# First token chunk multiplied among the last queries, token operands in two buffers of their own

## The chip, the cores and the metric

One core of one Trainium2 chip runs the whole program. The metric is the device time of one execution in microseconds; of several runs the median is given. A profiled execution of the same program supplies the trace.

## The reference, cut to what matters

Attention with random features, then a dense mixture of experts on its output. All matrices are float32.

```python
# q, k, v: (4, 8, 576, 64); omega: (128, 64); x: (2304, 512); w_gate: (512, 8)
# w1: (8, 512, 1024); w2: (8, 1024, 512)
h = einsum('bhsd,md->bhsm', x, omega) - sum(x*x)/2;  phi = exp(h - max(h)) / sqrt(m)
kv = einsum('bhsm,bhsd->bhmd', phi(k), v);  z = sum_s phi(k)
attn = einsum('bhsm,bhmd->bhsd', phi(q), kv) / (phi(q) . z + 1e-6)
x = attn reshaped to tokens x 512
P = exp(x @ w_gate - max);  8 times: P /= P.sum(1); P /= P.sum(0); P *= N / E
out = sum over e of P[:, e] * (relu(x @ w1[e]) @ w2[e])
```

## The kernel before, in words

**Attention.** A list of 36 jobs (lines 695 to 699) goes through keys, then keys mixed with queries, then the last queries. Each job is a generator; after each job is put in, `tick()` (L722) advances every open job by one stage. A stage is some 128-column transposes, matmuls of 65 to 256 columns, one or two PSUM evacuations on ScalarE (ACT) and some VectorE (DVE) work. The raw inputs lie in the pool `rw`, with three buffers each for `q`, `k` and `v` (L286). When the jobs are all in, `while active: tick()` (L750) lets the last queries run out.

**Token operands.** There are 18 tiles of 128 tokens in three chunks of six. When a chunk's six tiles stand in `xf`, `token_operands` (L98) makes seven operands for a seven-product (Strassen-like) 2x2 scheme, in the order 1, 5, 6, 3, 7, 2, 4 (`ORDER`). For each it forms a difference in place where one is needed (L107, on GpSimd (POOL) for chunks 0 and 1, on DVE for chunk 2), casts the high part on ACT (L122), takes the low part on DVE (L123), stores the pair to DRAM (L125, 768 KB), multiplies four of the seven by the gate weights `wgs` (`logits`, L147) and yields. The tile it writes is one of the four `xs` buffers (`token_tile`, L95). For chunk 2, whose tokens come last, the same tile is at once multiplied by the first expert's weights.

**Experts.** Sixteen units, each half an expert's hidden width. `first(u, c, i, g)` (L528) is a piece of the first product: six matmuls of 384 columns (L555) for one operand and one half of the weights, evacuated for each pair of pieces (L569 to L574). `second(s, i)` (L631) is six matmuls of 256 columns (L641) and one evacuation. A step `s` handles two token tiles: seven `second` calls, with pieces of later chunks taken from the list `todo` between them, five, five and four in three successive steps (L783). Left operands of a step come from `left_operands_a` and `left_operands_b` (L594, L610), on ACT and DVE. `split(u, w, i)` (L188) makes the high and low parts of a weight quarter: a difference on POOL (L194), a cast on ACT (L224), the low part on DVE or POOL (L225).

**The order of chunks.** The first unit takes chunk 2 first, from the buffers, then 0 and 1 (`order`, L506). Every later chunk's operands are read back from DRAM into `xs` by `load_next` (L514, L525), one for each pair of pieces done, four ahead.

**Between the two.** After the attention, left operands of step 0 are made, the query pool `sc` is closed, its memory goes to the pool `op_` (weight parts of the second product and the output tiles), four loads are issued (L759) and seven `split(0, 2, i)` follow (L761). `sc` lies on the side of memory that `op_` takes over, and `wgs` lies in `sc`. The pool `rw` gives its memory to `hp` (left operands and hidden tiles), the two PSUM banks of the key sums go to `px` (accumulators of `first`).

**What sets the order.** Line 825 builds the program with `schedule_with_timeline_sim=True`: a planner orders each engine's instructions by the order in the source and by when it thinks that each is ready. On the chip every engine, and the SP queue that issues the transfers, then works through its own list in order. Semaphores hold an instruction back until its inputs and its buffer are there.

Of the kernel before, what the change touches and what calls it, by code (L numbers as in the profile page):

```python
# [9 lines left out]
F32 = mybir.dt.float32  # L10
# [12 lines left out]
def moe_attention_kernel(  # L23
# [29 lines left out]
    P = 128  # L53
# [3 lines left out]
    SM = JM * P  # L57
    SR = S - SM
    XSB = 4
    RES = ()  # L60
    FB = 4
    NFB = FF // P // FB
# [35 lines left out]
    def token_operands(c, x):  # L98

        def q(r, h):  # L100
            h = 1 - h
            return x[:, 2 * r : 2 * r + 2, h * HL : (h + 1) * HL]

        last = c == NCH - 1

        def sub(o, a, b):
            (nc.vector if last else nc.gpsimd).tensor_tensor(o, a, b, op=ALU.subtract)  # L107

        for i in ORDER:
            if i == 5:
                sub(q(0, 0), q(0, 1), q(0, 0))
            elif i == 6:
                sub(q(0, 0), q(1, 1), q(0, 0))
            elif i == 7:
                sub(q(0, 1), q(1, 1), q(0, 1))
            elif i == 4:
                sub(q(0, 0), q(1, 0), q(0, 0))
            o = {3: q(1, 1), 7: q(0, 1), 2: q(1, 0)}.get(i, q(0, 0))  # L120
            t = token_tile()
            nc.scalar.copy(t[:, 0], o)  # L122
            nc.vector.tensor_tensor(t[:, 1], o, raw(t[:, 0]), op=ALU.subtract)  # L123
            xdram[c, i] = xd.tile([P, 2, 2, HL], F32, name=f"xd{c}_{i}")
            nc.sync.dma_start(out=xdram[c, i], in_=raw(t))  # L125
            logits(c, i, t)
            if last:
                xop[0, c, i] = t
                first(0, c, i, 0)
                first(0, c, i, 1)  # L130
            yield


    lpb = {}
# [127 lines left out]
    def load(which, key):  # L262

        src = {"q": q, "k": k, "v": v}[which]
        is_v = which == "v"
        if key[0] == "r":
            pr = key[1]
            rows = [(slice(i * SR, (i + 1) * SR), 2 * pr + i) for i in range(2)]
            if is_v:
                ts = []  # L270
                for i, (r, b) in enumerate(rows):
                    t = rw.tile([P, H + 1, D], F32, tag=f"vr{i}", bufs=1, name=f"vr{i}")
                    nc.gpsimd.memset(t, 0.0)
                    nc.gpsimd.memset(t[r, H, :], 1.0)
                    nc.sync.dma_start(out=t[r, :H, :], in_=src[b, :, SM:S, :].rearrange("h p d -> p h d"))
                    ts.append(t)
                rawt[which, key] = ts
            else:
                t = rw.tile([P, H, 1, D], F32, tag=f"{which}r", bufs=1, name=f"{which}r")
                for r, b in rows:  # L280
                    nc.sync.dma_start(out=t[r, :, 0, :], in_=src[b, :, SM:S, :].rearrange("h p d -> p h d"))
                rawt[which, key] = t
            return
        b, half = key
        view = src[b, :, :SM, :].rearrange("h (p j) d -> p h j d", j=JM)[:, :, 2 * half : 2 * half + 2, :]
        t = rw.tile([P, H + is_v, 2, D], F32, tag=which, bufs=3, name=which)  # L286
        if is_v:
            nc.gpsimd.memset(t[:, H], 1.0)
        nc.sync.dma_start(out=t[:, :H], in_=view)
        rawt[which, key] = t  # L290
# [214 lines left out]
    steps = [(u, n) for u in range(len(units)) for n in range(NP)]  # L505
    def order(u):  # L506

        return [NCH - 1] + list(range(NCH - 1)) if u == 0 else list(range(NCH))

    chunks = [(u, c) for u in range(len(units)) for c in order(u)]  # L510
    hraw, hneg, ops, xop, xres, hacc = {}, {}, {}, {}, {}, {}
    loads = [(u, c, i) for u, c in chunks[1:] for i in ORDER]

    def load_next():  # L514

# [12 lines left out]
    def first(u, c, i, g):  # L528
# [38 lines left out]
        if g == 1 or both is None:  # L567
# [4 lines left out]
                nc.vector.tensor_tensor(o, src, o, op=ALU.add)  # L572
            else:
                nc.scalar.copy(o, src)  # L574
        if g == 1 and (u, c) != chunks[0] and i not in RES:
            load_next()

    def tiles_of(u, n):
# [168 lines left out]
    hp_.append(ctx.enter_context(tc.tile_pool(name="hp", bufs=1, side="right", reuse_waits="tile")))  # L747
    kv_cm.__exit__(None, None, None)
    px.append(ctx.enter_context(tc.tile_pool(name="px", bufs=1, space=bass.MemoryType.PSUM, side="right")))
    while active:  # L750
        tick()
    left_operands_a(0)
    left_operands_b(0)
    sc_cm.__exit__(None, None, None)
# [1 line left out]
    ps[0] = ctx.enter_context(tc.tile_pool(name="ps4", bufs=4, space=bass.MemoryType.PSUM))  # L756
    pz.append(ctx.enter_context(tc.tile_pool(name="pz", bufs=1, space=bass.MemoryType.PSUM)))
    op_ = ctx.enter_context(tc.tile_pool(name="op", bufs=1, reuse_waits="tile"))
    for _ in range(XSB):  # L759
        load_next()  # L760
    for i in ORDER:  # L761
        split(0, 2, i)

    gate = sinkhorn()
    todo = pieces[14:]
    for s, (u, n) in enumerate(steps):
        c = n // (CT // 2)
        more = u + 1 < len(units)
# [10 lines left out]
        for k, i in enumerate(ORDER):  # L779
            second(s, i)  # L780
            if more and (n, k) in W2AT:
                split(u + 1, 2, ORDER[W2AT.index((n, k))])
            if k < (5, 5, 4)[n % 3] and todo:  # L783
                pc = todo.pop(0)
                first(*pc)
                j = ORDER.index(pc[2])
                if pc[1] == order(pc[0])[-1] and pc[3] == 1 and pc[0] + 1 < len(units) and j + 1 < len(ORDER):
                    split(pc[0] + 1, 1, ORDER[j + 1])
            if i == 7 and s + 1 < len(steps):
                left_operands_a(s + 1)  # L790
            if k in (1, 4):
                next(gate, None)
# [37 lines left out]
```

## Time and profile before

| what | value |
|---|---|
| median of 3 runs (lowest to highest) | 1658.14 us (1658.12 to 1659.32) |
| the profiled execution's own time | 1652.41 us |
| its span, first to last instruction | 1650.6 us |
| mean granted TensorE clock | 0.997 |

PE is TensorE's matmuls, PEld its weight loads. The page's first part gives busy time by engine; the span in 40 slices shows that only the first slice lies visibly below the others for PE. For this change the stretch from 110 us to 262 us matters: the three bursts of token operands and the change from attention to experts. The views used are busy time by stretch, waits, the timeline of one engine, groups of instructions and transfers.

### The profile page before, as it was taken

The numbers are of one execution on the slowest core, as the hardware profiler recorded it, in microseconds if no ns is written. First come the engines' busy times: TensorE is split into PE (matmuls) and PEld (weight loads), VectorE is DVE, ScalarE is ACT, GpSimd is POOL, SyncE is SP. The second block draws the span as 40 slices with busy tenths as digits, with TensorE's granted clock in tenths as the row PEclk, the third lists the DMA queues.
The fourth block names the chain that finished last, engine by engine and source line by source line (L and its number), as shares of the span: only waits on it lengthen the run. The fifth ranks groups of instructions, "written<-read, shape, count | busy, mean of one in ns | idle before, by whom it ended". The sixth has DMA issues, their size and how long they took to land.

```text
span 1650.6 us, 30079 instructions
## 1 busy us (share of the span) xinstructions
PE 1617.2 (98%) x11610; PEld 1598.3 (97%) x11610; DVE 1430.6 (87%) x2903; ACT 785.4 (48%) x1408; POOL 276.4 (17%) x232
## 2 busy tenths in 40 slices
PE   7999999999999999999999999999999999999998
PEld 7899889999999999999999999999999999999998
DVE  7999779898879898889888898989898888889878
ACT  6877646444334344443444443434444444444332
POOL 7631131111102011111111120102111111101000
PEclk9999999999999999999999999999999999999999
DMA  9422577564666565666647565665666565655462
GB/s 251 128 78 103 211 274 242 196 225 170 235 208 202 207 212 199 217 216 210 223 166 260 167 226 194 220 209 211 203 219 213 208 227 184 215 189 192 173 227 80
DMA packets 102686, 329.72 MB, mean 200 GB/s; under 512 B 14480, under 2 KB 39056, under 8 KB 102544
## 3 DMA queue, kind: packets, MB, share of 16 engines
q1 hardware_dynamic: 102544, 327.79, 58.1%
q8 instruction: 93, 1.52, 0.4%
q14 instruction: 49, 0.40, 0.1%
HBM read 306.53 MB, written 21.23 MB: 199 GB/s over the span
## 4 chain that ended last, share of the span: by engine, by line
PE 87%; DVE 11%; ACT 1%; issue 1%; SPq 0%; DMA 0%; POOL 0%; ACTq 0%; DVEq 0%
PE hx L555 24%; PE x L641 22%; PE hz L555 18%; PE z L641 11%; PE w L641 6%; DVE out L661 2%; DVE sm L592 1%; PE np L434 1%; DVE bl L592 1%; DVE mx L348 1%; PE kv L364 1%; PE qp L411 1%; DVE sl L620 1%; DVE cn L351 1%; PE pp L342 1%; DVE wl L225 1%
## 5 line engine op out<-in xcount | busy, mean ns | idle before, releaser
L555 PE MATMUL hx<-xs,wh 128*128 128x384 f32 x1536 | 371.9, 336 | 0.4 <-DVE prob L162 0.3
L661 DVE SCALAR_TENSOR_TENSOR out<-x,prob,out 128x256 f32<-128x256 f32 x504 | 237.0, 477 | 65.2 <-PE x L641 63.7
L555 PE MATMUL hz<-xs,wh 128*128 128x384 f32 x1152 | 282.0, 337 | 0.0
L555 PEld LDWEIGHTS hx<-xs,wh 128*128 128x128 f32 x1536 | 269.1, 188 | 0.8 <-issue 0.5
L194 POOL TENSOR_TENSOR st<-st 128x512 f32<-128x512 f32 x80 | 132.1, 1652 | 710.5 <-DVE wl L225 705.8
L555 PEld LDWEIGHTS hz<-xs,wh 128*128 128x128 f32 x1152 | 203.3, 189 | 0.2
L555 PE MATMUL hx<-xs,wl 128*128 128x384 f32 x768 | 199.6, 336 | 0.0
L623 ACT ACTIVATE bh<-hr 128x512 fp32r<-128x512 f32 x144 | 91.2, 633 | 223.5 <-PE x L641 218.4
L661 DVE SCALAR_TENSOR_TENSOR out<-z,prob,out 128x256 f32<-128x256 f32 x252 | 120.3, 477 | 56.8 <-PE z L641 56.2
L619 ACT CAST sh<-sm 128x512 fp32r<-128x512 f32 x144 | 89.6, 622 | 142.3 <-PE z L641 101.4
L224 ACT CAST wh<-st 128x512 fp32r<-128x512 f32 x176 | 104.8, 621 | 103.0 <-PE hx L555 43.1
L555 PE MATMUL hz<-xs,wl 128*128 128x384 f32 x576 | 151.2, 336 | 0.0
L592 DVE SCALAR_TENSOR_TENSOR sm<-hr,sm 128x256 f32<-128x256 f32 x288 | 137.4, 477 | 2.6
L555 PEld LDWEIGHTS hx<-xs,wl 128*128 128x128 f32 x768 | 138.7, 188 | 0.0
L225 DVE TENSOR_TENSOR wl<-st,wh 128x512 fp32r<-128x512 f32 x169 | 121.8, 732 | 8.0 <-ACT wh L224 7.7
L592 DVE SCALAR_TENSOR_TENSOR bl<-hr,bh 128x512 fp32r<-128x512 f32 x144 | 118.3, 822 | 3.4 <-ACT bh L623 3.4
L641 PE MATMUL z<-wh,sh 128*128 128x256 f32 x576 | 118.0, 282 | 1.9 <-ACT sh L606 0.8
L641 PE MATMUL x<-wl,sh 128*128 128x256 f32 x576 | 118.2, 281 | 0.0
L641 PE MATMUL z<-wl,sh 128*128 128x256 f32 x576 | 116.9, 281 | 1.0 <-POOL wl L225 1.0
L641 PE MATMUL x<-wh,sh 128*128 128x256 f32 x576 | 117.1, 284 | 0.6 <-DVE out L661 0.6
L600 ACT ACTIVATE ah<-hr 128x256 fp32r<-128x256 f32 x144 | 60.4, 419 | 119.2 <-PE x L641 94.5
L641 PE MATMUL z<-wh,sl 128*128 128x256 f32 x576 | 115.2, 281 | 1.5 <-DVE sl L607 1.5
(149 smaller groups left out, 3717.9 us busy)
## 6 DMA issues: line engine op xcount, KB each, us to landing
xs<-xd SPq DMA_DIRECT2D x329, 768.0 KB, 4.4
st<-in_moe_w_dram SPq DMA_DIRECT2D x64, 512.0 KB, 5.0
xd<-xs SPq DMA_DIRECT2D x21, 768.0 KB, 4.2
k<-in_k_dram SPq DMA_DIRECT2D x8, 512.0 KB, 6.7
v<-in_v_dram SPq DMA_DIRECT2D x8, 512.0 KB, 5.6
q<-in_q_dram SPq DMA_DIRECT2D x8, 512.0 KB, 6.3
out_dram<-out SPq DMA_DIRECT2D x16, 256.0 KB, 2.4
kr<-in_k_dram SPq DMA_DIRECT2D x4, 128.0 KB, 7.2
```

The costliest lines, as they stand in the source:

```text
L194: nc.gpsimd.tensor_tensor(o, a, b, op=op)
L224: nc.scalar.copy(hi, o)
L225: (nc.vector if u > 0 or (w == 2 and i in (1, 6, 7, 4)) else nc.gpsimd).tensor_tensor(lo, o, raw(hi), op=ALU.subtract)
L342: nc.tensor.matmul(o, lhsT=th[:, a], rhs=om_hi, start=True, stop=False)
L348: nc.vector.reduce_max(mx, p3, axis=AX.X)
L555: nc.tensor.matmul(pb, lhsT=a[:, k, g * P : (g + 1) * P], rhs=x[:, b, k, :], start=i in (1, 5, 2) and j == 0, stop=j == len(prods) - 1, sk ...
L592: nc.vector.scalar_tensor_tensor(o, in0=a, scalar=0.0, in1=b, op0=ALU.max, op1=op)
L600: nc.scalar.activation(ah, a11, AF.Relu)
L619: nc.scalar.copy(sh, sm)
L623: nc.scalar.activation(bh, a[:, 1:], AF.Relu)
L641: nc.tensor.matmul(pb, lhsT=ops[s][i][a][:, f], rhs=wt[u, 2, i][b][:, f], start=bool(start) and j == 0, stop=j == len(prods) - 1, skip_gro ...
L661: nc.vector.scalar_tensor_tensor(o, in0=pb, scalar=prob[:, t, e : e + 1], in1=o, op0=ALU.mult, op1=ALU.add)
```

## The change

The operands of all three chunks are written from two `xo` buffers in the pool `sc`, and read back from DRAM into `xs`, chunk 0 first. `logits` for an operand is issued one stage after the operand. The raw `q` tiles get two buffers in place of three. The products of chunk 0 are issued one piece for each tick after the last job is in, fourteen in all, and six pieces of chunk 1 among the seven splits that follow. Steps 0 to 2 then take three, three and two pieces in place of five, five and four.

```diff
+    XO = 2
+    AHEAD = 6
...
+        waiting = []
         for i in ORDER:
...
-            t = token_tile()
+            t = sc.tile([P, 2, 2, HL], F32R, tag="xo", bufs=XO, name="xo")
             nc.scalar.copy(t[:, 0], o)
             nc.vector.tensor_tensor(t[:, 1], o, raw(t[:, 0]), op=ALU.subtract)
             xdram[c, i] = xd.tile([P, 2, 2, HL], F32, name=f"xd{c}_{i}")
             nc.sync.dma_start(out=xdram[c, i], in_=raw(t))
-            logits(c, i, t)
-            if last:
-                xop[0, c, i] = t
-                first(0, c, i, 0)
-                first(0, c, i, 1)
+
+            if waiting:
+                logits(*waiting.pop())
+            waiting.append((c, i, t))
             yield
+        logits(*waiting.pop())
+        yield
...
-        t = rw.tile([P, H + is_v, 2, D], F32, tag=which, bufs=3, name=which)
+        t = rw.tile([P, H + is_v, 2, D], F32, tag=which, bufs=2 if which == "q" else 3, name=which)
...
-        return [NCH - 1] + list(range(NCH - 1)) if u == 0 else list(range(NCH))
+        return list(range(NCH))
...
-    loads = [(u, c, i) for u, c in chunks[1:] for i in ORDER]
+    loads = [(u, c, i) for u, c in chunks for i in ORDER]
...
-        if g == 1 and (u, c) != chunks[0] and i not in RES:
+        if g == 1 and i not in RES:
             load_next()
...
+    for _ in range(XSB):
+        load_next()
+    todo = list(pieces)
     while active:
         tick()
+        if len(todo) > len(pieces) - 14:
+            first(*todo.pop(0))
+    while len(todo) > len(pieces) - 14:
+        first(*todo.pop(0))
     left_operands_a(0)
     left_operands_b(0)
...
-    for _ in range(XSB):
-        load_next()
-    for i in ORDER:
+    for j, i in enumerate(ORDER):
         split(0, 2, i)
+        if j < AHEAD:
+            first(*todo.pop(0))
 
     gate = sinkhorn()
-    todo = pieces[14:]
...
-            if k < (5, 5, 4)[n % 3] and todo:
+            if k < ((5, 5, 4) if s > 2 else (3, 3, 2))[n % 3] and todo:
```

## Rows read from the trace of the kernel before

**Rows 1.** The page's first part: busy us, share, instructions of each engine.
```profile
PE 1617.2 (98%) x11610; PEld 1598.3 (97%) x11610; DVE 1430.6 (87%) x2903; ACT 785.4 (48%) x1408; POOL 276.4 (17%) x232
```
**Rows 2.** By stretch: length, busy PE, PEld, DVE, ACT, POOL (instructions), clock, DMA, GB/s.
```profile
110.00:132.00 22.00, 20.38 (x167) 18.73 (x166) 20.54 (x45) 15.09 (x33) 8.11 (x4) 1.00 0.58 220
...
186.80:217.90 31.10, 27.87 (x144) 25.32 (x145) 21.89 (x32) 16.45 (x26) 4.11 (x3) 0.89 0.93 361
217.90:234.00 16.10, 13.09 (x76) 12.38 (x75) 13.53 (x19) 9.08 (x18) 8.45 (x6) 0.89 0.68 250
234.00:262.00 28.00, 27.59 (x191) 27.24 (x190) 26.04 (x51) 16.61 (x35) 7.17 (x5) 1.00 0.72 246
262.00:1640.00 1378.00, 1371.00 (x9700) 1363.23 (x9698) 1198.79 (x2346) 603.20 (x1011) 176.70 (x113) 1.00 0.59 204
```
**Rows 3.** PE's waits from 176 to 262 us: total, times, longest.
```profile
PE lp L147 <- ACT xs L122: 1.5, 1, 1.5
PE z L641 <- DVE sl L607: 1.5, 1, 1.5
PE z L641 <- POOL wl L225: 1.0, 1, 1.0
```
**Rows 4.** Two stretches of 2 us: length, PE busy (matmuls), granted clock, DMA.
```profile
192.00:194.00 2.00, 0.92 (x3) 0.50 0.81 332
...
224.00:226.00 2.00, 2.00 (x8) 0.50 0.01 3
```
**Rows 5.** Timeline of PE where it runs dense: start, us, instructions.
```profile
227.36 0.51 PE L555 MATMUL hx<-xs,wh 128*128 128x384 f32 x2
...
229.45 0.39 PE L641 MATMUL x<-wl,sh 128*128 128x256 f32 x2
...
230.15 0.39 PE L641 MATMUL x<-wh,ah 128*128 128x256 f32 x2
```
**Rows 6.** Matmuls of L555 alone by stretch; the group of L147 in 186.8:217.93.
```profile
186.80:217.90 31.10, 18.71 (x96) 0.89 0.93 361
217.90:234.00 16.10, 8.26 (x38) 0.89 0.68 250
...
L147 PE MATMUL lp<-xs,wgs 128*128 128x384 f32 x28 | 8.0, 396 | 2.3 <-ACT xs L122 1.5 <-DVE xs L123 0.6
```
**Rows 7.** Timeline of ACT: first operand of chunk 1, last copy into xf, first w2 cast.
```profile
120.54 3.03 ACT L122 CAST xs<-xf 128x768 fp32r<-128x768 f32 x4 [1.93 <-POOL xf L107]
...
176.66 0.83 ACT L122 CAST xs<-xf 128x768 fp32r<-128x768 f32 x1
...
191.58 0.58 ACT L461 COPY xf<-xp 128x512 f32<-128x512 f32 x1 [0.47 <-PE xp L459]
...
214.19 0.61 ACT L224 CAST wh<-st 128x512 fp32r<-128x512 f32 x1
```
**Rows 8.** Line 123 by itself; the stores of L125, issue to landing; loads in 176:234.
```profile
L123 DVE TENSOR_TENSOR xs<-xf,xs x21: 944/951/2486, 110.9 to 208.0; 128x768 fp32r<-128x768 f32 x21
...
DMA to landing us min/median/max: 3.2/4.2/7.0
...
xs<-xd SPq DMA_DIRECT2D x8, 768.0 KB, 6.1
```
**Rows 9.** Timeline of PE: the last product of the tokens with the gate.
```profile
210.35 0.44 PE L147 MATMUL lp<-xs,wgs 128*128 128x384 f32 x1
```
**Rows 10.** Timeline of POOL, first and last of six entries on w2 parts.
```profile
216.24 2.99 POOL L194 TENSOR_TENSOR st<-st 128x512 f32<-128x512 f32 x2 [26.59 <-DVE wl L225]
...
229.13 1.29 POOL L225 TENSOR_TENSOR wl<-st,wh 128x512 fp32r<-128x512 f32 x1
```
**Rows 11.** Timelines of PE and SP: transposes of q tiles, the last q load.
```profile
147.50 0.60 PE L327 MATMUL tp<-ident,q 128*128 128x128 f32 x4
...
159.53 0.60 PE L327 MATMUL tp<-ident,q 128*128 128x128 f32 x4
...
128.40 0.38 SPq L289 DMA_DIRECT2D q<-in_q_dram  x1
```

## The prediction

> **What bounds the kernel now.** I read the page's first part first: PE is busy 98% of the span [rows 1]. Busy time by stretch then tells where the rest is. From 262 us on PE is busy 1371 of 1378 us [rows 2], so the long run of experts is bound by PE, and the change moves nothing there but the order of chunks in the first unit. What can move lies before 262 us, and there a busy PE is not a dense PE, so I count matmuls instead. Where PE runs dense, twelve matmuls of 384 columns take 229.45 - 227.36 = 2.09 us, 0.174 us each, and six of 256 columns take 230.15 - 229.45 = 0.70 us, 0.117 us each [rows 5]. A piece of the first product is thus 1.04 us, a `second` call 0.70 us. Transposes I take at 0.11 us, an estimate a little under the 0.117.
>
> In the stretch 186.8 to 217.9 us, the end of attention and the operands of chunk 2, 96 matmuls of L555 and 28 of L147 at 0.174 make 21.6 us, the other 20 of 144 at 0.11 make 2.2 us [rows 2, 6]. Together 23.8 of 31.1 us, so **7.3 us are lost**. Stretch 217.9 to 234.0, where the second product begins: 38 at 0.174 and 38 at 0.117 make 11.0 of 16.1 us, so **5.1 us are lost** [rows 2, 6]. The waits show how: the gate product waits for the ACT cast and the first second products wait for the DVE and POOL parts [rows 3]. The waits themselves are small; a good part of the loss is the clock, which fell to a granted 0.50 (1.2 of 2.4 GHz) after these gaps, so that only 3 matmuls ran in one stretch of 2 us and 8 in another [rows 4]. Both losses together, 12.4 us, are what the change can win. The burst of chunk 0 (110 to 132 us) has 22.0 - 20.38 = 1.6 us of idle PE besides [rows 2].
>
> **The change part by part.**
>
> *Products of chunk 0 among the last queries.* No matmul is added or removed; 14 pieces of 1.04 us, 14.6 us of PE work, need nothing of the last tokens and stand ready while the token chain runs. From 186.8 us the change has, beside the attention's rest, 28 gate products (4.9 us), 20 other matmuls (2.2 us) and 20 pieces (14 and the six ahead, 20.9 us): 28.0 us of dense work, to 214.8 us. The pieces that go in earlier push attention back by as much, and the sum stays. Cover is about twice the 7.3 us that it is to fill. I leave 1.5 us of that loss, as much as the gate product's longest wait for its cast [rows 3], between nothing and twice that. `logits` one stage late costs nothing of itself: eight small matmuls more or less ahead of it on PE are the cover.
>
> *Two buffers for 21 operands.* A tile's buffer is free when its store has landed. A round is cast 0.83 us [rows 7], low part 0.95 us [rows 8] and landing 4.2 us (3.2 to 7.0) [rows 8]: 6.0 us for two tiles, between 5.0 and 8.8. Chunk 1 starts at 176.66 us [rows 7]. The last gate product belongs to the 13th tile of chunks 1 and 2, that is after six rounds: 176.7 + 36 = 212.7, and with cast, low part and four gate products (0.7 us) 215.2 us. Before, it ended at 210.8 [rows 9]. The last xf copy at 192.2 [rows 7] lies earlier than the buffers allow (six to seven tiles of chunk 1, to about 197 us), so the buffers set the pace. Who waits for it: `wgs` lies in the memory that the w2 parts take, so the first w2 cast, 214.19 us before [rows 7], moves behind 215.2; with 0.62 us for it and a low part of at most 0.95 us the first `second` call runs at 216.5. PE's dense work ends at 214.8: **1.7 us idle** (at a landing of 3.2 us none, at 5.6 us about 11).
>
> The Trainium skill, DMA: Bandwidth & Descriptors, section Anatomy of one DMA, fits a transfer as a fixed 2.0 us, mostly the write's receipt, plus its bytes at 436 GB/s. For 768 KB that is an estimate of 3.8 us, by which the sum would win 1.7 us more; it is a fit for another issuing path, the trace's median is 4.2 us, and the row is used.
>
> *The handover.* POOL's work on the w2 parts ran from 216.24 to 230.42 us, 14.2 us [rows 10], and it stays whole. I let it begin at 217 and take 12 us, since the left operands of step 0, which shared those microseconds with it, can now be made while the six pieces run. PE has in that time 42 matmuls of `second` (4.9 us), three pieces (3.1 us) and what the planner draws forward of steps 1 and 2 (up to five pieces, 5.2 us): between 0 and 4 us idle, **2 us taken**.
>
> *Steps 0 to 2 with 8 pieces in place of 14.* PE's work in them falls by 6.2 us, DVE's hardly: DVE was busy 26.0 of 28 us in 234 to 262 [rows 2]. It can set the pace there; but the first left operands have gone ahead of it. Between 0 and 3 us, **1 us taken**.
>
> *Loads.* Seven loads of 768 KB more, in chunk 0's name, land 6.1 us after issue [rows 8]; four have tens of microseconds ahead of the first piece, the rest come one for each two pieces. On SP a load that waits for a pair of pieces stands ahead of later stores; that goes into the landing's range. The burst of chunk 0: later gate products against a slower two-buffer pace, 0 taken, from 1.6 us won to the price of the third rival.
>
> *Two q buffers.* The load of the last q tile now waits for the transposes at 147.50 in place of going at 128.40; the landing of 6 to 7 us lies ahead of its own first transpose at 159.53 [rows 11]. Nothing, at most 2 us through its squares. The `rw` and `px` memory is given over as before.
>
> The sum: 12.4 - (1.5 + 1.7 + 2.0) - 1.0 = **6.2 us won**. The profiled execution took 1652.41 us, 1.8 us more than its span and 5.7 less than the median; I carry the difference over: 1646.2 for a profile, 1652.0 as the median.
>
> **The rivals.**
> 1. *Full cover.* The stores land in 3.2 us and the planner draws pieces of steps 1 and 2 forward: losses of 0.5 to 1.5 us remain and the change wins 11 us, 1647. For it: PE's work only has to be in another order. Against it: POOL's 14.2 us.
> 2. *Even.* From 176 us on there are 14 stores and some eight loads in flight, and DMA was busy 0.93 of that stretch already [rows 2]. At a landing of 5.6 us a round is 7.4 us, the last gate product ends at 223.6, PE idles about 10 us of which up to 5.2 are filled: 1.5 + 5 to 10 + 2 + 1 against 12.4, a gain of -2 to 3, 1658. The case that the planner does not put the pieces among the queries, so that only the handover gains, gives 1655.5 and stands here too.
> 3. *Slower: the buffers hold ACT.* ACT works in order. In chunk 0's burst it ran four casts in a row in 3.03 us [rows 7]; with two buffers these take two rounds, 12 us. If the planner still puts them before the queries' evacuations, because it thinks that a store lands sooner than it does, ACT is held 9 us in each of the bursts of chunks 0 and 1, and half to all of that reaches PE: 9 to 18 us against 6.2, 1661 to 1670. It decides from about 1 us for each of the ten casts of these two chunks. Against it: the planner knows of the buffers and has other ACT work to put between. The Trainium skill speaks on this side: Perfetto Trace Analysis, section Optimization Strategy, takes the same gap repeating on the engine that should be saturated as a sign of too few buffers. No row of before shows such a gap with four.
>
> **How the numbers follow.** A measurement of this kernel tells 0.2%, 3.3 us, from no change. My forecast of 3.5 to 9 us won has 0.45, full cover 0.20, the even case 0.19, the slower one 0.16. So faster 0.65, same 0.19, slower 0.16. The range goes from 1645, the best of full cover, to 1661, the least of the third rival with the forecast's unknown costs at their upper ends; left out is most of the third rival and a little of the first.
>
> **What would show it.** Right: matmuls of L555 from about 175 us among transposes and token products; a granted clock of 1.00 through 186 to 234; a first `second` call at 215 to 218 with 20 pieces done; the stretch to 262 us holding some 36 matmuls of L555 more than before. Casts of operands waiting for stores (a wait on the transfer) by about 3 us a tile would show the buffers' pace. Wrong: PE idle over 5 us ahead of the first w2 parts (second rival), or PE's matmul count falling in 110 to 186 us with ACT waiting for stores (third). Were PE dense to 262 us and the time the same, my count of losses would be at fault.

## The result and the profile after

The changed kernel took 1677.95 us (median of four runs, 1677.26 to 1679.34) against 1658.13 for the kernel before on the same chip: a ratio of 1.0127, 95% interval 1.0116 to 1.0139. It is **slower by 20 us** and lies outside the predicted range (1645 to 1661). The profiled execution took 1677.52 us with a span of 1675.7. In two of the experiments below (without the gate products; six pieces ahead in the kernel before) one execution took over twice as long as the others (4039.59 and 3844.50 us), and the ratios leave these two out.

The page's first part of the kernel after [rows 1 of before]:

```profile
PE 1628.0 (97%) x11610; PEld 1604.1 (96%) x11610; DVE 1429.5 (85%) x2903; ACT 784.4 (47%) x1408; POOL 274.9 (16%) x232
```

The number of matmuls is the same, 11610. The added time is therefore idle PE or slow PE. Busy time by stretch, with the columns and the stretches of [rows 2]:

```profile
110.00:132.00 22.00, 21.46 (x189) 20.63 (x188) 21.21 (x49) 16.22 (x39) 7.31 (x4) 1.00 0.56 201
186.80:217.90 31.10, 26.58 (x200) 24.33 (x198) 17.84 (x39) 17.17 (x30) 7.33 (x4) 0.99 0.81 311
217.90:234.00 16.10, 12.86 (x35) 9.79 (x35) 6.34 (x8) 4.55 (x6) 0.00 (x0) 0.50 0.74 276
234.00:262.00 28.00, 22.60 (x122) 20.20 (x123) 19.19 (x32) 12.23 (x25) 9.85 (x7) 0.81 0.80 277
262.00:1640.00 1378.00, 1367.92 (x9647) 1359.64 (x9647) 1199.49 (x2337) 607.38 (x1025) 183.59 (x118) 1.00 0.60 205
```

The third row is to be seen first: in 217.9 to 234 PE counts as busy for 12.86 of 16.1 us, but it finishes 35 matmuls where the kernel before finished 76, at a granted clock of 0.50 (1.2 of 2.4 GHz).

To compare kernels I price every matmul as the prediction does (0.174 us for 384 columns, 0.117 for 256, 0.11 for the others [rows 5]) and take the sum from the stretch. What remains is **lost time**; a value a few us below zero means that small matmuls cost less than 0.11 there. Over the whole span it is 66.3 us before and 91.4 after; since the matmuls are the same, the difference is that of the spans, 25.1 us. (A matmul that crosses an edge counts on both sides of it, so stretches do not add up to the last tenths. The profiled execution of before lay 5.7 us under its median, so 25.1 is more than the 20 us between the medians.) By stretch, in us:

| stretch | before | after |
|---|---|---|
| 110 to 132 | 2.1 | -0.1 |
| 132 to 186.8 | -2.6 | 3.3 |
| 186.8 to 217.9 | 7.3 | 3.5 |
| 217.9 to 234 | 5.0 | 10.2 |
| 234 to 262 | 0.9 | 10.1 |
| 262 to 300 | 0.0 | 4.1 |
| 300 to 700 | 7.9 | 10.7 |

The stretch that the products were to fill did gain 3.8 us; the one ahead of it and all that follow lost more. Taken in one piece, 132 to 300 us went from 11.7 to 31.8 us lost. This last number is the one by which I compare the experiments' traces.

ACT's timeline of the kernel after shows the chain that sets this: first operand of chunk 1, then of chunk 2's operands, then the first w2 cast [rows 7]. In brackets is the wait just before.

```profile
187.60 0.83 ACT L124 CAST xo<-xf 128x768 fp32r<-128x768 f32 x1
...
218.06 0.83 ACT L124 CAST xo<-xf 128x768 fp32r<-128x768 f32 x1 [2.31 <-DMA xd<-xo]
...
233.25 0.83 ACT L124 CAST xo<-xf 128x768 fp32r<-128x768 f32 x1 [4.39 <-DMA xd<-xo]
235.09 0.83 ACT L124 CAST xo<-xf 128x768 fp32r<-128x768 f32 x1 [1.01 <-DVE xo L125]
239.28 0.83 ACT L124 CAST xo<-xf 128x768 fp32r<-128x768 f32 x1 [0.74 <-DMA xd<-xo]
244.45 0.80 ACT L577 COPY hr<-hz 128x768 f32<-128x768 f32 x1 [3.82 <-PE hz L558]
245.15 0.62 ACT L227 CAST wh<-st 128x512 fp32r<-128x512 f32 x1
```

The first cast of chunk 1 comes at 187.60 in place of 176.66, the 13th tile of chunks 1 and 2 at 235.09, and the first w2 cast at 245.15 in place of 214.19. That last cast stands on ACT behind the evacuation of a piece, which waits 3.82 us for a PE at half clock.

PE's timeline of the kernel after, gate products (L150) and first `second` call [rows 9]:

```profile
208.31 1.71 PE L150 MATMUL lp<-xo,wgs 128*128 128x384 f32 x8
...
218.95 2.00 PE L150 MATMUL lp<-xo,wgs 128*128 128x384 f32 x4 [3.75 <-ACT xo L124]
...
226.28 2.06 PE L150 MATMUL lp<-xo,wgs 128*128 128x384 f32 x4 [0.43 <-ACT xo L124]
...
235.97 2.00 PE L150 MATMUL lp<-xo,wgs 128*128 128x384 f32 x4 [2.43 <-ACT xo L124]
...
247.49 0.39 PE L644 MATMUL x<-wh,ah 128*128 128x256 f32 x2
```

Four gate products take 2.0 us (0.50 each), where eight took 1.71 at full clock. By 208 us the products of chunk 0 were used up (84 matmuls of L558, all fourteen pieces), 36 of these matmuls before 188 us. What stands between the gate products after that is one pair of pieces of chunk 1 each, twelve matmuls: the pair from 221.65 us on takes 4.2 us, twice what the prediction priced. Ahead of the first `second` call 144 matmuls of L558 ran, 24 pieces.

The waits of 176 to 262 us, kernel after (total, times, longest), and the stores of L127 issued in that stretch, issue to landing [rows 3, 8]:

```profile
ACT xo L124 <- DMA xd<-xo: 12.3, 6, 4.4
...
PE lp L150 <- ACT xo L124: 7.8, 4, 3.7
...
DMA to landing us min/median/max: 3.2/5.1/8.9
```

ACT waits 12.3 us for stores to give an operand buffer back, and PE waits 7.8 us for ACT's cast. Before, no cast of these chunks waited for a store, and the stores of that stretch landed in 4.2 us in the median. SP's timeline of the kernel after shows what the stores meet:

```profile
205.25 3.57 SPq L528 DMA_DIRECT2D xs<-xd  x2
209.03 3.48 SPq L127 DMA_DIRECT2D xd<-xo  x2
...
219.92 2.18 SPq L127 DMA_DIRECT2D xd<-xo  x2
```

The store issued at 209.03 went out behind two loads of chunk 1 and gave its buffer back to the cast at 218.06, 9.0 us later.

### The profile page after: what moved, and what is told of

Same layout as the page of the kernel before. It is cut to its first block, busy times and chain, and to the rows that moved or that the text cites. A ratio compares the mean times of both kernels' runs of the same rounds, so it can differ in the third digit from the quotient of the medians.

```text
span 1675.7 us, 30118 instructions
## 1 busy us (share of the span) xinstructions
PE 1628.0 (97%) x11610; PEld 1604.1 (96%) x11610; DVE 1429.5 (85%) x2903; ACT 784.4 (47%) x1408; POOL 274.9 (16%) x232
## 4 chain that ended last, share of the span: by engine, by line
PE 83%; DVE 12%; DMA 3%; ACT 1%; issue 1%; POOL 0%; SPq 0%; ACTq 0%; DVEq 0%
PE hx L558 22%; PE x L644 22%; PE hz L558 17%; PE z L644 11%; PE w L644 5%; DMA xd<-xo 2%; DVE out L664 1%; DVE sm L595 1%; DVE mx L351 1%; PE np L437 1%; DVE wl L228 1%; DVE bl L595 1%; DVE cn L353 1%; DVE cn L354 1%; DVE sl L623 1%
## 5 line engine op out<-in xcount | busy, mean ns | idle before, releaser
L558 PE MATMUL hx<-xs,wh 128*128 128x384 f32 x1536 | 374.6, 337 | 1.0 <-DMA xs<-xd 0.7
L558 PE MATMUL hz<-xs,wh 128*128 128x384 f32 x1152 | 283.6, 339 | 3.7 <-DVE hr L575 1.5
L558 PEld LDWEIGHTS hx<-xs,wh 128*128 128x128 f32 x1536 | 269.9, 189 | 2.1 <-DMA xs<-xd 1.2
L558 PEld LDWEIGHTS hz<-xs,wh 128*128 128x128 f32 x1152 | 204.1, 190 | 5.6 <-DVE hr L575 2.1
L558 PE MATMUL hx<-xs,wl 128*128 128x384 f32 x768 | 199.1, 336 | 0.0
L558 PE MATMUL hz<-xs,wl 128*128 128x384 f32 x576 | 152.1, 338 | 0.0
L558 PEld LDWEIGHTS hx<-xs,wl 128*128 128x128 f32 x768 | 139.0, 189 | 0.0
L644 PE MATMUL x<-wh,sl 128*128 128x256 f32 x576 | 116.8, 282 | 0.0
```

The costliest lines, as they stand in the source:

```text
L558: nc.tensor.matmul(pb, lhsT=a[:, k, g * P : (g + 1) * P], rhs=x[:, b, k, :], start=i in (1, 5, 2) and j == 0, stop=j == len(prods) - 1, sk ...
L644: nc.tensor.matmul(pb, lhsT=ops[s][i][a][:, f], rhs=wt[u, 2, i][b][:, f], start=bool(start) and j == 0, stop=j == len(prods) - 1, skip_gro ...
```

## The experiments

**My theory** after this reading: two buffers make each pair of operands wait for its stores, the stores share the transfers with chunk 1's loads, and the products of chunk 0 are spent before the gaps open. **Rivals:** the gate products in PE's order hold everything behind them; the pieces among the queries do the harm; the moved pieces of steps 0 to 2 or the third q buffer cost it; or the order of chunks does, whatever the buffers. The last one has no run of its own: none has the new order with four buffers. "Lost" below is lost PE time from 132 to 300 us in the run's trace: 11.7 before, 31.8 after. The ratios are those on record to the kernel before on the same chip, not quotients of the medians, and runs are compared by them; 0.1% is 1.7 us. The number in brackets behind a ratio is its 95% interval.

### First group: one part taken out of the change

Without the gate products (their softmax works on zeros, so the output's weights are left out):

```diff
-            if waiting:
-                logits(*waiting.pop())
-            waiting.append((c, i, t))
...
-        logits(*waiting.pop())
+    nc.gpsimd.memset(prob, 0.0)
```

> The changed kernel without the products of the tokens with the gate weights in all three chunks (their results are set to zero, so the mixture weights are those of equal logits); 60 matmuls of 384 columns, 10 us of dense PE work, fall away. Theory (PE stands still because a gate product, which waits for an operand that waits for a buffer, is ahead of ready pieces in PE's order): the pieces run freely, the clock stays at 1.00 from 200 to 245 us, and the time falls by the 10 us and by 15 us or more of stalls, to 1653 or less. Rival (the second product is late anyway, because the operands hold the memory of the w2 parts): the stall only moves behind the pieces, the first second product still comes at about 245 us, and the time falls by the 10 us or less, to 1667 to 1672.

1672.66 us, ratio 1.0086 (1.0060 to 1.0112). Sixty matmuls, 10.4 us of work, were gone, and the time fell by 0.41%, 6.8 us; lost time rose to 39.6. The gate products were not the holder. The waits of 176 to 262 us in this run:

```profile
ACT xo L125 <- DMA xd<-xo: 30.2, 9, 9.8
...
PE hz L555 <- DMA xs<-xd: 9.0, 3, 6.0
...
PE x L641 <- ACT wh L224: 5.5, 2, 4.5
```

ACT's wait for stores grew to 30.2 us, and PE then waited for chunk 1's loads and the w2 casts; the first `second` call came at 241.33 us. The stall only moved, as the rival said.

Three operand buffers; the memory comes from one of the two `sq` buffers (squares of queries and keys), and the second run is its control:

```diff
-    XO = 2
+    XO = 3
...
-        s = sc.tile([P, H, n, D], F32, tag="sq", bufs=2, name="sq")
+        s = sc.tile([P, H, n, D], F32, tag="sq", bufs=1, name="sq")
```

> The changed kernel with three operand buffers in place of two; the memory comes from the squares, one buffer in place of two (see the next run for that alone). Theory (the buffers set the pace of the operands while a store takes 4 to 9 us to land): a third buffer takes a third of the wait out of the chain; the casts of chunk 2 come at 3 us or less a tile, the last gate product some 8 to 12 us earlier than 238 us, and the time is 8 to 14 us under the next run's. Rival (transfers are full from 203 to 219 us, so that any number of buffers waits for the same bytes): within 4 us of the next run.

```diff
-        s = sc.tile([P, H, n, D], F32, tag="sq", bufs=2, name="sq")
+        s = sc.tile([P, H, n, D], F32, tag="sq", bufs=1, name="sq")
```

> The changed kernel with one buffer for the squares in place of two and nothing else, the control of the run before. Both theories: the squares' waits cost 0 to 4 us, 1678 to 1682.

Three buffers: 1667.52 us, 1.0067 (1.0047 to 1.0086), lost 25.3. The control: 1670.38 us, 1.0081 (1.0061 to 1.0101), lost 25.1. The third buffer by itself is worth 0.14%, 2.3 us, here, and the two intervals overlap: the theory of 8 to 14 us **falls**, and the rival holds. The control was a surprise that neither theory allowed for: taking a buffer away made the changed kernel 0.46%, 7.6 us, faster. Its trace has another order of the instructions ahead of 187 us, and it loses nothing in 132 to 176 us (-0.3) where the changed kernel loses 3.1.

Two q buffers alone, in the kernel before:

```diff
-        t = rw.tile([P, H + is_v, 2, D], F32, tag=which, bufs=3, name=which)
+        t = rw.tile([P, H + is_v, 2, D], F32, tag=which, bufs=2 if which == "q" else 3, name=which)
```

> The kernel before with two buffers for the raw queries in place of three and nothing else. Theory (the loss is in the operands' chain after 200 us): 0 to 3 us slower, 1658 to 1661. Rival (ACT waits for the late query tiles, the attention runs slower, and the clock falls at 130 to 150 us): 4 to 8 us slower, 1662 to 1666.

1658.93 us, 1.0023 (1.0010 to 1.0037), 3.8 us slower. Lost time is 12.8 in 132 to 300, near that of before, but 13.3 in place of 7.9 in 300 to 700 us. I come back to this in the fourth group.

The pieces of chunk 0 only after the last tick:

```diff
     while active:
         tick()
-        if len(todo) > len(pieces) - 14:
-            first(*todo.pop(0))
```

> The changed kernel with the fourteen pieces of chunk 0 issued after the last tick in place of one for each tick. Theory (in PE's order ready pieces stand behind gate products that wait, and chunk 0's loads crowd the stores): the token chain now runs without loads of its own making and ends earlier, but PE has nothing beside it; 1670 to 1682, near the changed kernel. Rival (the pieces among the queries hold up the attention and so the tokens): the first operand of chunk 1 comes at 177 to 181 us in place of 187.6, and the time falls by 8 us or more, to 1670 or less.

1670.32 us (1667.4 to 1676.0), 1.0088 (1.0068 to 1.0108), lost 30.4: 0.39%, 6.5 us, faster than the changed kernel, and over half of the loss stays. The trace shows that this is not the rival's reason. The planner drew 36 matmuls of L558 ahead of 188 us here too, and the first operand of chunk 1 came at 188.63 us, not at 177 to 181. What changed stands behind that: the other eight pieces came after the operands, and chunk 1's loads with them; no load of operands was issued between 186.4 and 232.1 us. The stores of 176 to 262 us in this run:

```profile
DMA to landing us min/median/max: 3.2/3.3/4.2
```

The 13th tile came 35.3 us after the first, 5.9 us a round of two tiles, against 7.9 in the changed kernel. The run speaks of loads among stores, and does not show what pieces among the queries cost.

### Second group: the small parts by themselves

`logits` one stage late in the kernel before; six pieces among the splits (and 3, 3, 2 after) in the kernel before; both; and the change without the six pieces:

```diff
-            logits(c, i, t)
+            if waiting:
+                logits(*waiting.pop())
+            waiting.append((c, i, t))
...
+        logits(*waiting.pop())
```

> The kernel before with each gate product issued one stage later and nothing else. Theory (PE's waits for the cast ahead of the gate products, 2 to 3 us and the low clock behind them, are avoided): 1 to 5 us faster, 1653 to 1657. Rival (the planner had placed them by readiness already): within 1.5 us, 1657 to 1660.

```diff
+    todo = pieces[14:]
     for j, i in enumerate(ORDER):
         split(0, 2, i)
+        if j < 6:
+            first(*todo.pop(0))
...
-            if k < (5, 5, 4)[n % 3] and todo:
+            if k < ((5, 5, 4) if s > 2 else (3, 3, 2))[n % 3] and todo:
```

> The kernel before with six pieces of its second chunk issued among the seven splits of the second product's weights, and three, three and two in the first three steps; nothing else. Theory (the 5 us lost while POOL and DVE make those parts can be covered): 2 to 5 us faster, 1653 to 1656. Rival (the operands are still being loaded then, and the steps become bound by DVE): no change or up to 4 us slower, 1658 to 1662.

> The kernel before with both: gate products one stage later and six pieces among the splits. Theory: the two gains add, 4 to 9 us faster, 1649 to 1654. Rival: they cover the same stall, and the better of the two alone is not beaten by more than 1 us.

```diff
-    AHEAD = 6
+    AHEAD = 0
...
-            if k < ((5, 5, 4) if s > 2 else (3, 3, 2))[n % 3] and todo:
+            if k < (5, 5, 4)[n % 3] and todo:
```

> The changed kernel without the six pieces among the splits, and with five, five and four pieces in the first three steps as before. Theory (DVE sets the pace of steps 0 to 2 when they hold only eight pieces; PE waited 2.1 us and ran at 1.2 GHz for some microseconds behind that): the loss of 4 us from 262 to 300 us goes, but PE stands emptier ahead of the second product, 4 to 6 us more; in sum within 4 us of the changed kernel. Rival (six pieces out of PE's order let the second product begin sooner): 5 us or more faster, 1673 or less.

The ratios are 0.9992 (0.9980 to 1.0004), 0.9995 (0.9985 to 1.0004), 0.9997 (0.9987 to 1.0007); the change without the six pieces took 1678.29 us, 1.0137 (1.0124 to 1.0150). Neither part can be measured in the kernel before, alone or together. The last run tests nothing: its trace has the matmuls, the work of ACT, DVE and POOL and the transfers in the same order as the changed kernel, from first to last. As far as the trace tells, the planner made the same program of both sources, so this run is a repeat of the changed kernel, and shows what its time and its trace scatter by (1.0137 and 1.0127; lost 32.4 and 31.8).

### Third group: loads and buffers in the new order

Chunk 1's loads held back until the last operand of chunk 2 is written (a copy of two elements ties them to it); then the same with three buffers and one `sq`:

```diff
-        if g == 1 and i not in RES:
+        if g == 1 and i not in RES and not (u == 0 and c == 0 and loads[0][1] == 1):
             load_next()
...
+            if after is not None:
+                nc.vector.tensor_copy(xop[u, c, i][:, 0, 0, 0:2], raw(after)[:, 1, 1, HL - 2 : HL])
...
+    for _ in range(XSB):
+        load_next(last_t[0])
```

> The changed kernel with the loads of chunk 1's operands held until the last token operand of chunk 2 is written (four tiny copies tie them to it, 0.2 us of DVE each); chunk 0's loads and everything else as in the change. Theory now (the first runs showed that a third buffer wins only 3 us; while chunk 0's pieces free their buffers, chunk 1's loads go in between the stores, and a store that lands in 4 us alone takes 7 to 9 us): the stores of chunk 2 land in 3.2 to 4.5 us, the casts come at about 3 us a tile, the last cast at 220 to 226 us in place of 239.3, and the time falls by 8 to 14 us, to 1664 to 1670. Rival (two buffers and one store's own landing are the pace, loads or not): the last cast stays past 230 us, and, since the first pieces of chunk 1 now wait for late loads, the time is 1676 to 1684.

> The loads held as in the first run of this group, and three operand buffers (memory from the squares, one buffer for two). Theory (without the loads a third buffer counts): casts of chunk 2 at 2 to 2.5 us a tile, the last cast some 5 to 8 us earlier than with two buffers, and 3 to 7 us faster than it. Rival (the casts are then bound by the tokens, not by buffers): within 2 us of the run with two.

Loads held: 1670.89 us, 1.0100 (1.0087 to 1.0112), 0.27%, 4.5 us, better than the change; lost 29.9. With three buffers besides: 1662.79 us, 1.0046 (1.0033 to 1.0059), lost 23.3, another 0.54%, 8.9 us. One `sq` buffer is within it, and by itself that was worth 0.46% in the changed kernel; with loads held it has no control, so what the third buffer adds here is not shown. ACT's waits and the landing of the stores of 176 to 262 us, loads held:

```profile
ACT xo L124 <- DMA xd<-xo: 6.0, 3, 2.5
...
DMA to landing us min/median/max: 3.2/3.3/4.3
```

and with three buffers besides:

```profile
ACT xo L124 <- DMA xd<-xo: 2.6, 2, 1.5
```

ACT's wait for stores falls from 12.3 to 6.0 and to 2.6 us, and a round from 7.9 to 6.2 and 5.8 us. The wait is no measure of the time, though: with one `sq` alone (1.0081) it is 13.0 us, with the pieces after the ticks (1.0088) 13.6. While the loads run, buffer and `sq` together win 0.60% and the held loads alone 0.27%; both together 0.81%.

### Fourth group: buffers in the old order

The kernel before with operands in two, then three buffers of their own (q in two; the second also with one `sq`), and its control with one `sq` alone:

```diff
-            t = token_tile()
+            t = sc.tile([P, 2, 2, HL], F32R, tag="xo", bufs=2, name="xo")
```

> The kernel before, with its order of chunks and chunk 2 multiplied from the buffers where it stands, but all operands in two buffers of their own and two buffers for the raw queries; no other part of the change. Theory (buffers wait for stores, whatever order the chunks have): each tile of chunk 2 waits for the store two tiles back and for its two pieces, 3 to 4 us a tile in place of 2; 5 to 10 us slower than the kernel before, 1662 to 1667, of which the queries' buffers alone gave 2 to 5. Rival (two buffers hurt only together with the loads of chunk 0 and 1): within 3 us of the run with the queries' two buffers alone, 1657 to 1661.

> The old order with operands in three buffers of their own (two query buffers, one buffer for the squares). Theory (the number of buffers is what counts): 5 to 9 us faster than with two, 1660 to 1665. Rival (the operands' separate memory, and what is laid over it later, is what counts): within 3 us of the run with two buffers, 1667 to 1672.

> The kernel before with one buffer for the squares and nothing else, the control for the memory of the third buffer. Theory: squares have time, within 3 us of the kernel before, 1654 to 1661. Rival (one buffer sorts the squares better, as the earlier control on the changed kernel came out 7 us faster): 4 us or more faster, 1652 or less.

Two buffers: 1669.82 us (1665.2 to 1673.3), 1.0082 (1.0066 to 1.0098), lost 19.8. Three: 1658.06 us, 1.0011 (1.0000 to 1.0023), lost 11.8, as before. One `sq` alone: 1658.64 us, 1.0013 (1.0004 to 1.0023). So in the old order, too, two buffers cost 13.6 us with the q buffers in it, and one buffer more takes back 11.8; one `sq` alone makes the old kernel no faster. The traces place 8.0 of the 11.8 us in 132 to 300 us (19.8 against 11.8 lost) and 4.1 ahead of 132 us, where traces scatter that much. The price does not show as waits on the transfer: ACT waits 2.5 us for stores of 176 to 262 us with two buffers and 2.2 with three. It shows in when the casts stand: six rounds take 37.9 us with two buffers (6.3 each) and 30.2 with three. PE in 200 to 220 and 220 to 245 us with two buffers (columns as in [rows 4], then GB/s):

```profile
200.00:220.00 20.00, 17.10 (x75) 0.82 0.62 251
220.00:245.00 25.00, 20.91 (x120) 0.93 0.58 221
```

and with three:

```profile
200.00:220.00 20.00, 19.43 (x112) 1.00 0.67 273
220.00:245.00 25.00, 22.43 (x141) 0.93 0.69 232
```

One more buffer and PE finishes 58 matmuls more in these 45 us.

The two small prices, 0.23% for two q buffers and 0.13% for one `sq`, have one and the same place. PE's waits in 300 to 700 us, two q buffers alone:

```profile
PE w L641 <- DVE bl L592: 2.0, 3, 1.3
PE x L641 <- DVE out L659: 1.7, 2, 1.2
```

and one `sq` alone:

```profile
PE w L641 <- DVE bl L592: 2.0, 3, 1.3
PE x L641 <- DVE out L659: 1.7, 2, 1.2
```

Two different edits give the same rows in a stretch in which neither tile exists any more (before, the first of these waits is 1.4 us and the second 0.4). It is not a wait for q: from 300 to 690 us the two traces have DVE's instructions in the same order but for one, and the kernel before has them in another. That either edit tips the planner into this order is read from the traces; it was not tried by itself.

### Fifth group: the cover

The pieces of chunk 0 issued in pairs with chunk 2's operands and tied to them (zero times the operand is added to two elements of `xo0`, the tile read back from DRAM), so that they cannot be spent earlier; then the same with held loads, three buffers and one `sq`:

```diff
             waiting.append((c, i, t))
+            if last:
+                xo0 = xop[todo[0][0], todo[0][1], todo[0][2]]
+                nc.vector.scalar_tensor_tensor(xo0[:, 0, 0, 0:2], in0=raw(t)[:, 0, 0, 0:2], scalar=0.0, in1=raw(xo0)[:, 0, 0, 0:2], op0=ALU.mult, op1=ALU.add)
+                first(*todo.pop(0))
+                first(*todo.pop(0))
...
         tick()
-        if len(todo) > len(pieces) - 14:
-            first(*todo.pop(0))
```

> The changed kernel with each pair of chunk 0's pieces issued at, and tied to, an operand of chunk 2 (a copy of two columns that adds zero times the operand to chunk 0's, 0.2 us of DVE, seven times), so that they can't run ahead of it. Theory (the cover was spent ahead of the gap): chunk 1's first operand comes at about 181 us in place of 187.6, PE has 2.1 us of pieces beside each operand of chunk 2 and keeps the full clock for most of 205 to 240 us, and the time falls by 8 to 14 us, to 1664 to 1670. Rival (the operands set the pace whatever stands beside them; pieces done early are not lost, only moved): within 4 us of the changed kernel, 1674 to 1682.

> Pieces tied as in the run before, the loads of chunk 1 held until the last operand, and three operand buffers (one buffer for the squares). Theory (three causes that add: buffers, loads between stores, cover spent early): 1652 to 1660, about the kernel before. Rival (they cover the same stall; the third mend gives nothing over the two of the earlier run at 1662.8): 1661 to 1665.

Tied alone: 1679.36 us, 1.0140 (1.0125 to 1.0154), lost 32.0: nothing won. ACT's waits and PE's, 176 to 262 us:

```profile
ACT xo L124 <- DMA xd<-xo: 17.5, 7, 6.3
...
PE hx L563 <- DVE xs L134: 6.1, 1, 6.1
```

The pieces now wait for the operands, and the operands for their stores (17.5 us). No piece stands ahead of 188 us, and the first operand of chunk 1 comes at 179.87, 7.7 us sooner than in the changed kernel, the first `second` call at 238.99, 8.5 sooner; the time is the same. My theory that the early spending of the cover was a cause by itself **falls**: with two buffers and loads in flight, pieces in the right place idle just as long. With loads held and three buffers, the tie gives 1660.93 us, 1.0027 (1.0016 to 1.0037), lost 18.3, against 1.0046 without it: 0.19%, 3.1 us, with intervals that just overlap. No version was faster than the kernel before.

## Why the prediction was wrong

**Where time can be lost** was right: before 262 us lay 7.3 and 5.0 us, and only 2.8 of the 25.1 us of added loss arose between 300 and 700 us. The long run of experts did not change its pace.

**Products among the last queries** was half right. The stretch from 186.8 to 217.9 went from 7.3 to 3.5 us lost, where I had left 1.5. But the sentence "The pieces that go in earlier push attention back by as much, and the sum stays" was followed by "Chunk 1 starts at 176.66 us", and the two can't both hold. The planner put 36 of the 84 matmuls ahead of 188 us. Before, PE had nothing idle in 132 to 176; so 6.3 us of pieces (36 by 0.174), 3.9 us of new loss in that stretch (from -0.8 to 3.1) and 0.7 us ahead of it pushed the first operand of chunk 1 to 187.60. PE's sum stayed; the start of the chain behind it did not. This is the first step that failed: the chain began 10.9 us later, and 36 of the matmuls that were to stand beside it were done. The tied runs show the pieces' part: with none ahead, the chain began 7.7 and 7.1 us sooner than in the same kernel without the tie. They also show that this part alone does not decide the time (1.0140 tied, 1.0127 not).

**Two buffers** is the second. I took 6.0 us for a round, from a landing of 4.2. (At a landing of 5.6 my own sum gives 10.1 us of idle PE, as in the second rival, not "about 11".) Six rounds took from 187.60 to 235.09, 7.9 us each: 11.5 us more in all. In the first three, to 207.17, no cast waited for a store; there the last queries, with the pieces among them, set the pace (19.6 us for five tiles), where I had put the buffers' pace ahead of theirs. From there to 239.28 the stores did, 32.1 us for eight tiles: the stores of 176 to 262 us landed in 5.1 us in the median, those among loads in up to 8.9. I had named the loads, but put them into the landing's range.

Without loads among the stores the sum holds: at a landing of 3.3 us cast, low part and landing make 5.1 us, and with the pieces after the ticks the rounds that wait for stores take 5.2, all six 5.9 each. But with such rounds (5.9, and 6.2 with loads held) the kernel is still 0.88 and 1.00% slower: the late start stays, the cover is used early or stands behind the operands, and PE waits for casts at the gate products (13.4 and 8.1 us of 188 to 262 us). A chain at the predicted pace was thus not covered as the prediction has it, with 1.7 us of idle PE.

Start and rounds together put the 13th tile 22.4 us late. The Trainium skill, Perfetto Trace Analysis, section Optimization Strategy, says that the same gap repeating can mean too few buffers. The runs agree in the old order, where a third buffer gives back 11.8 us; in the new order, with 12.3 us of waits on stores and loads running, it gives 2.3, not clear of noise.

**The first `second` call** came at 247.49, 31.0 us after the predicted 216.5: those 22.4 us, and then the last gate products at half clock (2.0 us) and a w2 cast behind a piece's evacuation that waited 3.82 us for PE. I had priced 1.7 + 2.0 us of idle time; the two stretches from 217.9 to 262 lost 20.3 us, where they had lost 5.9. The clock was read in [rows 4] as part of what could be won, and never as a price: the granted clock was 0.50 from 218 to 244 us. I had also expected some 36 matmuls of L555 more by 262 us; there were 36 fewer (180 against 216).

**The planner drawing pieces forward as cover** did happen: 24 pieces stood ahead of the first `second` call, four more than the order of the source puts there (and as many where the source has no six pieces among the splits). The last four ran from 240.16 and 245.30 us on, behind the last gate product, in what was left of the wait for the w2 parts; the gaps ahead of them were open already.

**Steps 0 to 2** had the mechanism right and the size low. 262 to 300 us lost 4.1 us where I took 1, at most 3. In 270 to 280 DVE was busy all 10 us (columns as in [rows 2]):

```profile
270.00:280.00 10.00, 8.18 (x47) 8.18 (x48) 10.00 (x21) 6.95 (x14) 4.31 (x3) 0.83 0.08 28
```

The run that was to test this had no edit that reached the chip, but the others speak for it: what goes with the loss is how many pieces the planner had put ahead of the first `second` call, and so taken from the steps. With 18 to 30 ahead (24 in the kernel after) the stretch lost 4.1 to 5.8 us, with 14 ahead 0.2 to 2.0. This is a comparison across runs, not a run of its own.

**Two q buffers** I took as 0, at most 2; alone they cost 3.8 us, not by the wait I had weighed. **Late `logits`** at nothing was right (0.9992).

**The rivals.** The second, "Even", named the mechanism (landing by loads and stores together, PE idle ahead of the w2 parts), and its sign of failure, PE idle over 5 us ahead of the first w2 parts, is what the trace shows; it set up to 5.2 us of filling against it; four such pieces came, and the stretch lost 20.3 us all the same. The third, ACT held by the buffers, came true for chunks 1 and 2, in six waits of up to 4.4 us. In chunk 0's burst 110 to 132 us lost 2.2 us less than before, but the burst now runs on: its last two casts, at 136.45 and 140.49, waited 0.46 and 0.68 us for stores, and one gate product waited 2.0 us for the first of them.

That is where the 3.9 us of new loss ahead of 176 us begin. PE in 132 to 138 and 138 to 142 us:

```profile
132.00:138.00 6.00, 3.97 (x44) 1.00 1.00 356
138.00:142.00 4.00, 4.00 (x25) 0.60 0.97 366
```

Ahead of that cast ACT had also waited 1.47 us for a q tile that landed among these transfers (DMA was busy all the time); before, PE was busy for all of 132 to 142.

**What stays open.** The parts don't add up cleanly: the buffers and q cost 0.82% in the old order, the new order adds 0.45%, of which held loads alone take back 0.27 and pieces issued behind the ticks alone 0.39. With three buffers, held loads, tied pieces and one `sq` 0.27% remains; the trace places it at 200 to 245 us (12.6 us lost, 5.5 in the old order with three buffers). PE's waits of 176 to 262 us in that run are 5.3 us for casts and low parts of gate products, 2.6 for the tying instruction itself and 3.1 for w2 parts; which of them makes the rest was not tried. How much of what these runs win belongs to one `sq` is not shown either, since every run in the new order with three buffers has it. Why it makes the changed kernel 0.46% faster and the old one 0.13% slower is not settled; 3.4 us of the gain stand at 132 to 176 us, where the planner gives another order. The cause of the loss is thus shown in part: two buffers by themselves in the old order, loads among the stores in the new one; how the rest divides between the late start, the spent cover and the order is argued.

## What to carry to other kernels

Work that fills a gap must be checked against the start of the chain that makes the gap: pieces put into a stretch where PE was dense delayed that chain here by about their length (6.3 us of pieces; 7.1 and 7.7 us without them) and were gone when the gap came. A buffer that is held until its store has landed costs write plus landing for each round (5.2 us measured at a landing of 3.3, 5.1 by the sum), and the landing to use is that of stores among the loads which the same change adds, not the median of a quieter run. Before an experiment's time is read as the price of what was edited, its trace must show that the edit did what was meant: the planner moved the same pieces forward without being told to, it made the same program of two sources, and one buffer less for an unrelated tile gave another order. Price a stall on PE at both clocks: the matmuls behind it took 0.35 us here in place of 0.174 until the clock was back.

## What the runs showed of the hardware

With two buffers and no load of operands going out beside it (loads held, or pieces after the ticks) a store of 768 KB landed in 3.2 to 4.3 us. Among loads of the same size it took up to 8.9 us in the kernel after, and the median of the fourteen stores of 176 to 262 us rose from 3.3 to 5.1. The lines stand above.

A stall of PE had a long price: in the kernel after, PE stood idle for 3.75 us ahead of the gate product at 218.95. PE by stretch:

```profile
216.00:218.00 2.00, 0.00 (x0) 0.83 1.00 381
...
224.00:230.00 6.00, 4.97 (x15) 0.50 0.54 138
...
240.00:244.00 4.00, 3.84 (x12) 0.50 0.98 401
...
246.00:250.00 4.00, 4.00 (x26) 1.00 0.73 269
```

From 218 to 244 us the granted clock was 0.50, and idle times of 0.4 to 2.4 us came between the groups of matmuls. Twelve matmuls ran in 4 us there; after 246, at 1.00, 26 did, four of them of 256 columns.

Ahead of 132 us the traces lose between 22.7 and 27.7 us. PE in the run without the six pieces (27.5):

```profile
50.00:60.00 10.00, 7.11 (x38) 0.71 0.39 117
```

and in the kernel after (23.5):

```profile
50.00:60.00 10.00, 8.75 (x76) 1.00 0.70 206
```

38 matmuls stand against 76, though the two programs run the same instructions in the same order. Such scatter is as large as several of the effects here, which is why lost time by stretch was compared, and not only spans.
